# PSUM as one buffer of eight banks, and a new order, in a fused recurrence and feed-forward kernel

## Chip, cores and metric

One NeuronCore of one Trainium2 chip runs the whole kernel. The metric is device time in microseconds. A profiled execution has a span (first to last instruction) and a time of its own, which is a little longer than the span.

## What is computed

Two stages. The first is a recurrence over 768 steps for 4 batches x 8 heads, each with a 40 x 40 state. The second is a feed-forward product on its output, 3072 tokens of 320 features, 2048 wide inside:

```python
for t in range(S):
    y[:, :, t] = einsum('bhd,bhde->bhe', rt, state)
    Sa = einsum('bhde,bhe->bhd', state, at)
    state = state * wt[:, :, None, :] - einsum('bhd,bhe->bhde', Sa, bt)
    state = state + einsum('bhd,bhe->bhde', vt, kt)
...
h = x @ w_in                 # 3072 x 320 by 320 x 2048
g = np.maximum(h, 0.0) ** 2
out = g @ w_out              # 3072 x 2048 by 2048 x 320
```

## The kernel before

The 768 steps are cut into 12 chunks of 64. Within a chunk the recurrence is worked as matrix products; only the state goes from one chunk to the next. For each chunk `c` the kernel plans named steps. The names matter below, since the order is a text of them:

- `prep`: logarithm of the decays (`ln`, `hi`, `lo`), their running sums on PE (`ci`, `cf`) and exponentials of these on ACT (`ei`, `ex`, `ec`, `ef`, `eg`); transposes of the inputs on PE (`TA`, `TR`, `TK`, and `Tk`, `Tb`, `TU` in chunks 0 to 3) with copies or products out of PSUM (`tA`, `tR`, `tK`, ...); the masked score matrix `EN` (PE) and `mEN` (DVE).
- `rec`: `AS`, `EV`, `NU` (PE) with `u0`, `u1` between them solve the chunk; `SC`, `S` and `s` make the new state, `TS` and `tS` turn it.
- `read`: `TV`, `tV`, `CX`, `mCX`, `RS`, `Y`, `y`, `yd`, `XT`, `xt` make the chunk's 256 tokens.
- `ffn`: four quarters `u0` to `u3` of the first product (`F` over 256 of the 320 features, `FL` over the last 64), the Relu `f`, the square `q`, and the second product. For chunks 0 to 10 the second product is four steps `O c u0` to `O c u3`, each of eight matmuls that alternate between the two banks of one buffer, one bank for each half of the tokens; one read `o c` of 640 columns empties both, and `st c` stores. Chunk 11 alone has the halves as steps of their own (`OL 11 u g`, emptied by `oe 11 g`).

PE writes into PSUM, and DVE or ACT must read each result out. PSUM's eight banks are four buffers of two banks each, with tags pb0 to pb3. A PE step that opens a result names its buffer in the order text (`PE3 O 0 u0`; a step that goes on in an open buffer is plain `PE`); everything that reads it goes through `slot` (line 330):

```python
slots[h] = ps.tile([128, 2, 512 if dt == FP32 else 1024], dt, name=f"pb{i}",
                   tag=f"pb{i}", bufs=1)
```

Nothing schedules at run time. `ORDER` (line 82) is one text of some 1050 entries, engine and step, and `Plan.issue` (line 52) emits the instructions in that order; each engine then works through its own in sequence. The framework places the semaphore waits: it compares what the instructions emitted so far read and write in each buffer, and makes a later instruction wait for an earlier one on another engine where the two touch the same part of a buffer and at least one writes, or where both are in PSUM.

The set `WIDE` names transposes and sums done as whole 128 x 128 matmuls; the others are done as pairs of 64-row matmuls that write the two banks of the pair. `flat` (line 499) shows a buffer's two banks as one row for the whole ones, and `sums` (line 505) does so for the exponentials that read `cf`. Entries such as `WD3` are fills: matmuls of constants whose result nobody reads, emitted by `fill` (line 1037).

Of the kernel before, what the change touches and what calls it, by code (L numbers as in the profile page):

```python
# [82 lines left out]
SP ldb 0; PE1 cf 0 h0; ACT castk 0; ACT ln 0 h1; SP lda 0; POOL castb 0; SP ldw 1; SP ldb 1; PE2 Tk
0; DVE hi 0 h1; DVE lo 0 h1; SP ldv 0; PE cf 0 h1; ACT eg 0; POOL castA 0; PE3 WD1; PE3 Tb 0; PE ci
0 h1; DVE tb 0 g0; SP ldk 1; ACT ef 0; ACT ln 1; SP ldr 0; SP lda 1; POOL hi 1; SP ldw 2; DVE tk 0
g0; ACT castb 1; PE1 WD3; PE1 TA 0; POOL lo 1; SP ldk 2; ACT ec 0; DVE tk 0 g1; DVE tb 0 g1; DVE tA
0 g0; DVE tA 0 g1; PE2 WD2; PE3 TU 0; ACT castV 0 g1; PE2 EN 0 g0; DVE mEN 0 g0; PE1 EN 0 g1; PE0
cf 1; POOL castV 0 g0; SP st0 0; POOL castk 1; DVE mEN 0 g1; PE2 ci 1; PE1 EV 0; ACT ec 1; DVE tU
0; PE2 Tb 1; DVE u0 0; PE3 Tk 1; ACT eg 1; PE NU 0; DVE tb 1 g0; POOL castR 0; POOL castA 1; SP ldv
1; ACT ef 1; DVE tb 1 g1; ACT u1 0 g0; SP lda 2; PE0 TR 0; SP ldr 1; ACT u1 0 g1; PE2 TA 1; ACT tR  # L90
0 g0; PE1 S 0 g0; DVE tk 1 g1; DVE tk 1 g0; DVE tA 1 g0; ACT tR 0 g1; PE S 0 g1; ACT ln 2; SP ldw
3; PE3 TV 0; DVE s 0 q1; PE0 EN 1 g0; DVE tA 1 g1; DVE s 0 q0; PE2 TU 1; DVE mEN 1 g0; ACT tV 0; SP
ldb 2; POOL hi 2; PE1 EN 1 g1; POOL lo 2; ACT castk 2; POOL castV 1 g0; DVE tU 1; SP ldv 2; PE3 cf
2; ACT eg 2; ACT ef 2; SP lwi 0 u1; PE0 CX 0 g1; PE2 AS 1; DVE mEN 1 g1; POOL castV 1 g1; PE EV 1;
PE1 CX 0 g0; ACT u0 1; POOL castA 2; PE3 ci 2; DVE mCX 0 g1; PE0 Tk 2; PE NU 1; DVE mCX 0 g0; ACT
ec 2; POOL castR 1; DVE tk 2 g1; DVE tk 2 g0; PE1 TA 2; PE3 TR 1; DVE tA 2 g0; PE0 SC 1; ACT u1 1
g0; POOL castb 2; SP ldk 3; POOL castV 2 g0; SP ldr 2; ACT u1 1 g1; PE2 Y 0; PE S 1 g0; DVE tA 2
g1; ACT ln 3; PE S 1 g1; PE1 TS 0; DVE y 0; DVE yd 0; ACT tR 1 g1; ACT tR 1 g0; DVE s 1 q0; SP ldw
4; SP lwi 0 u0; POOL hi 3; POOL castV 2 g1; DVE s 1 q1; PE2 Tb 2; DVE tb 2 g0; DVE tb 2 g1; PE3 TV
1; PE0 TS 1; PE2 TU 2; ACT tS 0; DVE tS 1; DVE lo 3; SP lwl 0; PE0 EN 2 g0; ACT tV 1; POOL cwi 0  # L100
u1; DVE mEN 2 g0; PE3 EN 2 g1; PE1 cf 3; DVE mEN 2 g1; PE0 CX 1 g1; ACT tU 2; POOL castk 3; PE2 AS
2; POOL castR 2; PE EV 2; PE3 CX 1 g0; ACT eg 3; ACT ef 3; PE1 XT 0; ACT u0 2; DVE mCX 1 g1; PE0 TR
2; PE NU 2; DVE mCX 1 g0; ACT tR 2 g0; PE3 ci 3; POOL cwi 0 u0; DVE xt 0; SP lwi 0 u2; ACT u1 2 g0;
ACT ec 3; PE1 F 0 u1; PE3 RS 1; PE Y 1; SP lwi 0 u3; ACT u1 2 g1; PE2 SC 2; DVE yd 1; PE S 2 g0;
POOL cwl 0; PE S 2 g1; DVE y 1; DVE s 2 q1; ACT tR 2 g1; ACT ln 4; PE3 XT 1; POOL cwi 0 u3; PE FL 0
u1; DVE xt 1; ACT f 0 u1; PE0 TV 2; DVE s 2 q0; ACT tV 2; PE3 Tk 3; PE1 F 1 u0; DVE tk 3 g1; DVE tk
3 g0; SP lda 3; PE2 TS 2; PE FL 1 u0; PE0 CX 2 g0; PE3 FL 0 u2; SP ldb 3; DVE tS 2; SP ldr 3; ACT
cwi 0 u2; DVE mCX 2 g0; PE F 0 u2; POOL hi 4; POOL lo 4; PE2 F 0 u3; SP lwo 0 x0; POOL castb 3; SP
ldv 3; SP lda 4; ACT castA 3; PE0 TA 3; SP lwo 0 x2; PE FL 0 u3; ACT f 1 u0; DVE f 0 u2; ACT f 0
u3; DVE tA 3 g0; POOL castR 3; PE1 FL 1 u2; DVE tA 3 g1; PE3 cf 4; PE F 1 u2; PE0 Tb 3; PE2 FL 1  # L110
u1; SP lwo 0 x1; DVE tb 3 g1; POOL castV 3 g0; ACT ef 4; ACT f 1 u2; POOL cwo 0 x0; POOL castV 3
g1; SP lwo 0 x3; ACT q 0 u2; PE3 CX 2 g1; PE F 1 u1; PE1 F 0 u0; ACT f 1 u1; PE FL 0 u0; DVE tb 3
g0; DVE mCX 2 g1; PE0 FL 1 u3; PE3 EN 3 g0; ACT f 0 u0; ACT q 0 u1; DVE mEN 3 g0; PE2 EN 3 g1; PE F
1 u3; POOL castA 4; SP lwo 0 x6; ACT f 1 u3; SP lwo 0 x5; DVE mEN 3 g1; ACT q 1 u0; PE1 TU 3; PE3
TR 3; PE2 AS 3; PE EV 3; POOL cwo 0 x1; PE0 ci 4 h1; DVE tU 3; DVE q 0 u0; ACT tR 3 g0; PE1 RS 2;
ACT u0 3; PE Y 2; PE NU 3; ACT ei 4 h1; DVE tR 3 g1; DVE y 2; DVE yd 2; ACT u1 3 g0; PE3 O 0 u0; SP
lwo 0 x4; PE1 SC 3; PE S 3 g0; SP lwo 0 x7; POOL q 1 u3; DVE u1 3 g1; PE S 3 g1; ACT ex 4 h1 g0;
DVE s 3 q0; SP ldw 5; PE2 ci 4 h0; DVE s 3 q1; ACT cwo 0 x2; ACT ex 4 h1 g1; POOL cwo 0 x3; SP ldb
4; POOL cwo 0 x6; PE0 XT 2; PE O 0 u1; ACT q 0 u3; SP ldk 4; ACT cwo 0 x4; PE1 TV 3; POOL cwo 0 x7;
ACT cwo 0 x5; ACT ex 4 h0 g1; ACT ei 4 h0; DVE xt 2; PE0 TA 4; PE O 0 u2; ACT ex 4 h0 g0; ACT ln 5;  # L120
PE O 0 u3; DVE tV 3; PE1 CX 3 g0; SP ldv 4; DVE tA 4 g0; DVE tA 4 g1; DVE hi 5; SP lda 5; POOL lo
5; PE0 TS 3; SP ldr 4; POOL mulKB 4 h0; POOL castV 4 g1; POOL castV 4 g0; ACT o 0; DVE mCX 3 g0; SP
lda 6; ACT q 1 u2; PE2 F 2 u0; POOL q 1 u1; PE FL 2 u0; PE1 FL 2 u1; PE F 2 u1; DVE tS 3; POOL
castR 4; ACT f 2 u0; PE0 FL 2 u3; PE2 CX 3 g1; DVE mulKB 4 h1; POOL castA 5; ACT f 2 u1; SP ldb 5;
PE3 ci 5 h1; ACT ei 5 h1; DVE mCX 3 g1; ACT ex 5 h1 g0; ACT ex 5 h1 g1; PE F 2 u3; PE1 TK 4; ACT f
2 u3; PE2 cf 5; ACT ef 5; DVE tK 4; PE3 F 2 u2; PE1 EN 4 g0; PE0 EN 4 g1; DVE mEN 4 g0; POOL q 2
u1; PE FL 2 u2; PE2 O 1 u0; DVE mEN 4 g1; PE1 RS 3; ACT f 2 u2; PE Y 3; PE3 AS 4; SP ldk 5; ACT q 2
u0; PE EV 4; PE O 1 u1; POOL q 2 u3; ACT q 2 u2; DVE yd 3; ACT u0 4; DVE y 3; SP ldw 6; PE1 ci 5
h0; PE0 XT 3; PE NU 4; PE O 1 u2; SP ldk 6; DVE u1 4 g0; PE O 1 u3; ACT ei 5 h0; ACT ex 5 h0 g1;
ACT u1 4 g1; DVE xt 3; PE3 TA 5; PE0 TR 4; ACT ex 5 h0 g0; POOL mulKB 5 h1; ACT o 1; ACT tR 4 g1;  # L130
SP ldr 5; DVE tA 5 g1; PE1 TV 4; PE2 SC 4; POOL mulKB 5 h0; PE S 4 g0; DVE tA 5 g0; PE S 4 g1; ACT
tR 4 g0; ACT ln 6; SP ldv 5; DVE tV 4; PE0 TK 5; DVE s 4 q1; PE3 FL 3 u3; PE F 3 u3; ACT tK 5; PE1
O 2 u0; DVE s 4 q0; ACT hi 6; ACT castR 5; PE0 CX 4 g0; PE2 CX 4 g1; POOL lo 6; SP ldb 6; PE O 2
u1; DVE mCX 4 g0; ACT f 3 u3; PE O 2 u2; ACT castV 5 g0; ACT q 3 u3; DVE mCX 4 g1; PE3 ci 6 h0; SP
st 0; ACT ei 6 h0; PE2 TS 4; PE0 EN 5 g1; ACT ex 6 h0 g0; PE O 2 u3; ACT ex 6 h0 g1; PE3 RS 4; DVE
tS 4; PE Y 4; PE2 EN 5 g0; DVE mEN 5 g1; PE0 cf 6; ACT o 2; PE1 ci 6 h1; DVE y 4; ACT ef 6; POOL
castV 5 g1; ACT ex 6 h1 g0; DVE yd 4; DVE mEN 5 g0; PE3 F 3 u2; PE0 F 3 u1; PE FL 3 u1; ACT ex 6 h1
g1; POOL castA 6; PE FL 3 u2; ACT ei 6 h1; DVE f 3 u1; PE1 XT 4; POOL mulKB 6 h0; PE2 AS 5; ACT f 3
# [942 lines left out]
```

## Time and profile before

| | us |
|---|---|
| three runs | 243.48, 244.87, 242.04 |
| median | 243.48 |
| the profiled execution, its own time | 242.46 |
| its span | 240.6 |
| POOL busy in it | 125.1 |
| squares on POOL (20) | 39.0 |
| squares on ACT (20) | 20.8 |

The page names engines PE (matrix products; PEld is the load of its stationary operand), DVE and ACT (which both read PSUM), POOL (which works in SBUF only) and SP (which issues the loads and stores). In a line of a group, the form is source line, engine, operation, what is written from what, shape, count, then busy time of all of them, the mean duration of one in ns, and the idle time that came just before, with what ended it. Matmuls are pipelined, so their mean duration is longer than their place in a stream, which is busy time by count. In a list of stretches, each row has the busy time of every engine, then the granted PE clock (1.00 is full speed), the share of DMA and its rate.

### The profile page before, as it was taken

How to read it: one execution, taken by the hardware profiler on the slowest of the kernel's cores; microseconds unless marked ns; L12 is line 12 of the kernel's file. 1: busy time of each engine (PE TensorE's matmuls, PEld its weight loads, DVE VectorE, ACT ScalarE, POOL GpSimd, SP SyncE). 2: the span in 40 equal slices, each digit the busy share in tenths (PEclk: the TensorE clock that was granted, in tenths of full speed). 3: DMA queues.
4: the chain of work that ended last, by engine and by line, in shares of the span. 5: the costliest groups of instructions: out<-in, count | busy, mean ns of one | idle time of the engine just before them, and what ended most of it. 6: DMA issues, size and time to landing. Idle time of an engine off the chain costs nothing.

```text
span 240.6 us, 12143 instructions
## 1 busy us (share of the span) xinstructions
PE 223.9 (93%) x5526; PEld 175.8 (73%) x5526; DVE 179.6 (75%) x227; ACT 176.3 (73%) x228; POOL 125.1 (52%) x126
## 2 busy tenths in 40 slices
...
PEclk9999999999999999999999999999999999999998
...
GB/s 99 208 232 180 225 169 207 277 248 177 315 120 174 187 115 172 224 183 158 173 172 151 177 178 178 131 44 126 161 116 6 4 3 23 94 3 3 57 0 108
DMA packets 100873, 33.55 MB, mean 139 GB/s; under 512 B 84950, under 2 KB 100822, under 8 KB 100822
## 3 DMA queue, kind: packets, MB, share of 16 engines
...
q8 instruction: 43, 0.70, 1.2%
...
## 4 chain that ended last, share of the span: by engine, by line
PE 68%; DVE 8%; issue 1%; ACT 1%; DVEq 0%
PE pb L379 36%; PE pb L893 23%; PE pb L383 7%; PE pb L387 2%; DVE STb L796 2%; DVE G L927 1%; DVE AR L679 1%; DVE VUT L360 1%; DVE EN L704 1%; DVE Yb L855 1%; DVE VU L362 1%; DVE CX L704 1%; ACT osb L365 0%; DVE KB L375 0%; ACT lnW L578 0%
## 5 line engine op out<-in xcount | busy, mean ns | idle before, releaser
L379 PE MATMUL pb<-WOUT,G 128*128 128x320 bf16 x384 | 56.8, 300 | 0.0
L929 POOL TENSOR_TENSOR G<-G 128x1024 bf16<-128x1024 bf16 x20 | 39.0, 1958 | 28.3 <-ACT G L921 28.1
L921 ACT ACTIVATE G<-pb 128x1024 bf16<-128x1024 f32 x40 | 40.6, 1022 | 15.4 <-PE pb L893 13.3
L893 PE MATMUL pb<-XT,WIN 128*128 128x256 bf16 x384 | 48.2, 273 | 0.5 <-issue 0.3
L379 PEld LDWEIGHTS <-G 128*128 128x128 bf16 x384 | 35.7, 98 | 14.2 <-issue 0.5
L893 PEld LDWEIGHTS <-WIN 128*128 128x128 bf16 x384 | 35.0, 98 | 8.4 <-issue 2.8
L373 POOL TENSOR_TENSOR KB<-raw_kb,iG 128x640 bf16<-128x640 f32 x14 | 21.7, 1552 | 31.7 <-ACT iG L620 23.7
L704 DVE TENSOR_TENSOR CX<-pb,MSKI 128x1024 bf16<-128x1024 f32 x24 | 28.7, 1218 | 5.8 <-PE pb L379 5.7
L704 DVE TENSOR_TENSOR EN<-pb,MSK 128x1024 bf16<-128x1024 f32 x24 | 28.7, 1217 | 3.8 <-PE pb L379 3.7
L931 ACT ACTIVATE G<-G 128x1024 bf16<-128x1024 bf16 x20 | 20.8, 1051 | 0.1
L796 DVE TENSOR_TENSOR STb<-pb,GT 40x640 bf16<-40x640 f32 x22 | 18.0, 820 | 2.3 <-PE pb L379 2.0
L373 POOL TENSOR_TENSOR lo<-lnW,hi 128x640 bf16<-128x640 f32 x10 | 14.0, 1399 | 9.7 <-ACT hi L365 5.0
L679 DVE TENSOR_TENSOR AR<-pb,GT 128x512 bf16<-128x512 bf16 x24 | 15.6, 684 | 3.2 <-PE pb L383 3.1
L893 PE MATMUL pb<-XT,WLAST 64*128 64x256 bf16 x192 | 17.5, 271 | 0.1
L379 PEld LDWEIGHTS <-EN 64*64 64x64 bf16 x768 | 14.2, 109 | 3.1 <-DVE EN L704 1.3
L923 DVE TENSOR_SCALAR G<-pb 128x1024 bf16<-128x1024 f32 x8 | 9.8, 1220 | 8.7 <-PE pb L893 8.6
L365 ACT ACTIVATE osb<-pb 128x640 f32<-128x640 f32 (+1 forms) x10 | 6.8, 677 | 12.3 <-PE pb L379 10.6
L855 DVE TENSOR_TENSOR Yb<-pb,Gin 128x640 bf16<-128x640 f32 (+1 forms) x24 | 12.4, 553 | 4.3 <-PE pb L379 4.2
L369 POOL CAST VU<-raw_v 64x640 bf16<-64x640 f32 x20 | 14.6, 734 | 1.3 <-DMA raw_v<-in_v_dram 0.7
L626 ACT ACTIVATE Gin<-pb 64x320 f32<-64x320 f32 x32 | 13.7, 428 | 1.5 <-PE pb L379 1.1
L653 ACT ACTIVATE GT<-pb 128x1024 f32<-128x1024 f32 x12 | 12.3, 1022 | 2.4 <-PE pb L379 1.9
L365 ACT ACTIVATE VU<-pb 64x640 bf16<-64x640 f32 x17 | 11.8, 696 | 2.9 <-DVE VU L362 1.6
...
## 6 DMA issues: line engine op xcount, KB each, us to landing
...
```

What stands on the lines that cost most here:

```text
L365: alts.append(("ACT", c_act(n), lambda: nc.scalar.activation(out=o_(), in_=i_(), func=ACTF.Copy, scale=1.0 if scale is None else scale)))
L373: return [("POOL", 40 + 2.35 * n, lambda: nc.gpsimd.tensor_tensor(out=o_(), in0=a_(), in1=b_(), op=op)), ("DVE", c_dve(n), lambda: nc.vect ...
L379: return lambda: nc.tensor.matmul(out=o_(), lhsT=l_(), rhs=r_(), start=start, stop=stop, skip_group_check=True)
L383: return lambda: nc.tensor.transpose(out=o_(), in_=i_(), identity=IDb[64 * g:64 * g + n, 0:n])
L679: ew(f"tA {c} g{g}", [("DVE", c_dve(512), lambda g=g: nc.vector.tensor_tensor(out=steps(AR[q2][:, 0, g]), in0=turned(ha, g), in1=steps(GT[ ...
L704: ew(f"m{nm} {c} g{g}", [("DVE", c_dve(1024), lambda: nc.vector.tensor_tensor(out=dst[q2][:, g].rearrange("p q i t -> p (q i) t"), in0=slo ...
L796: ew(f"s {c} q{q}", [("DVE", c_dve(2 * n), lambda q=q: nc.vector.tensor_tensor(out=STb[q2][live(q), :, q, 0:D], in0=slot(hs, FP32)[live(q) ...
L855: return [("DVE", c_dve(2 * (f1 - f0)), lambda: nc.vector.tensor_tensor(out=Yb[q2][:, :, to:to + f1 - f0], in0=slot(hy, FP32)[:, :, f0:f1] ...
L893: return lambda: nc.tensor.matmul(out=o_(), lhsT=l_(), rhs=r_(), start=begins and opens(hf, x), stop=ends and not opens(hf, x), skip_group ...
L921: ("ACT", c_act(1024), lambda gb=gb, hf=hf: nc.scalar.activation(out=gb, in_=slot(hf, FP32)[:], func=ACTF.Relu)),
L929: ("POOL", 1900, lambda gv=gv: nc.gpsimd.tensor_tensor(out=gv, in0=gv, in1=gv, op=ALU.mult)),
L931: ("ACT", c_act(1024), lambda gv=gv: nc.scalar.activation(out=gv, in_=gv, func=ACTF.Square))],
```

## The change

PSUM becomes one buffer `PB` of eight banks. A step that opens a result names one or two banks by digit: `PE14 CX 3 g1` takes banks 1 and 4, `PE2 OL 1 u0 g1` bank 2 alone. `pick_banks` makes the view, a stride over the bank axis for a pair that lies apart. Chunks 0 to 10 get their second product in halves as chunk 11 had it: `OL c u g`, each half in a bank of its own, and two reads `oe c g` of 320 columns in place of `o c`. Whole transposes of eight blocks fit one bank and take only one. `flat` goes, and views keep the bank as an axis of its own; the exponentials of whole sums (`cf` 0, 2, 3) are read in two halves of 512 columns, by bank. `WIDE` gains TA 3, TA 5, TA 7, TA 8, TR 4 and Tk 2, and loses TA 4, TU 3, TV 3 and cf 1. The order is new throughout, with other engines for some steps (squares: ACT 20 to 14, DVE 8 to 13, POOL 20 to 21; Relu: ACT 40 to 37, DVE 8 to 11; `mulKB` on DVE 2 to 3) and 32 fill matmuls where there were 6. Loads are issued on SP in a new order, and so are the stores.

```diff
-                self.fill(int(where[2:]), name[1], int(name[2:]))
+                self.fill([int(x) for x in where[2:]], name[1], int(name[2:]))
...
-                self.slot_of[h] = int(where[len(eng):])
+                self.slot_of[h] = sorted(int(x) for x in where[len(eng):])
...
+    PB = ps.tile([128, 8, 512], FP32, name="pb", tag="pb", bufs=1)
 
     def slot(h, dt):
 
         if h not in slots:
-            i = plan.slot_of[h]
-            slots[h] = ps.tile([128, 2, 512 if dt == FP32 else 1024], dt, name=f"pb{i}",
-                               tag=f"pb{i}", bufs=1)
-        return slots[h]
+            slots[h] = pick_banks(plan.slot_of[h])
+        return slots[h] if dt == FP32 else slots[h].bitcast(dt)
+
+    def pick_banks(x):
+        return PB[:, x[0]:x[-1] + 1:max(1, x[-1] - x[0]), :]
...
-    def flat(h, dt=BF16):
-        return slot(h, dt)[:].rearrange("p b x -> p (b x)")
+    def block(h, i, dt=BF16):
+        n = 4 if dt == FP32 else 8
+        return slot(h, dt)[:, i // n, 128 * (i % n):128 * (i % n) + 128]
...
+    def exp_sums(c, h, to, scale):
+        def go():
+            if wide_sums(c):
+                for x in range(2):
+                    nc.scalar.activation(
+                        out=to().rearrange("p (g b m) t -> p g b m t", g=2, b=2)[:, :, x],
+                        in_=slot(h, FP32)[:, x].rearrange("p (m g t) -> p g m t", g=2, t=L),
+                        func=ACTF.Exp, scale=scale)
+                return
...
         ho = ("O", c)
-        apart = c == NCH - 1
-
         def bank(g):
-            return slot(ho + (g,), FP32)[:, 0, 0:DM] if apart else slot(ho, FP32)[:, g, 0:DM]
+            return slot(ho + (g,), FP32)[:, 0, 0:DM]
...
-            if apart:
-                for g in range(2):
-                    pe(f"OL {c} u{u} g{g}", "D", DM, ms[g], reads=rd, writes=[ho + (g,)],
-                       alloc=[ho + (g,)] if u == 0 else [])
-            else:
-                pe(f"O {c} u{u}", "D", DM, [m for x in zip(*ms) for m in x], reads=rd,
-                   writes=[ho], alloc=[ho] if u == 0 else [])
+            for g in range(2):
+                pe(f"OL {c} u{u} g{g}", "D", DM, ms[g], reads=rd, writes=[ho + (g,)],
+                   alloc=[ho + (g,)] if u == 0 else [])
...
+        for g in range(2):
+            ew(f"oe {c} g{g}", copy_alts(lambda g=g: osb[q2][:, g, :], lambda g=g: bank(g), DM),
+               reads=[ho + (g,), ("left", c - 2)] + ([("osb", q2)] if c < 2 else []),
+               writes=[("osb", q2, g)], free=[ho + (g,)])
         if c < NCH - 1:
-            ew(f"o {c}", copy_alts(lambda: osb[q2][:], lambda: slot(ho, FP32)[:, :, 0:DM], 2 * DM),
-               reads=[ho], writes=[("osb", q2)], free=[ho])
...
     def fill(i, mode, n):
-        t = ps.tile([128, 2, 512], FP32, name=f"pb{i}", tag=f"pb{i}", bufs=1)
+        t = pick_banks(i)
```

A stretch of the new order, around the second product of chunk 4:

```
PE05 SC 6; PE37 RS 6; PE Y 6; ACT castV 8 g1; PE S 6 g0; PE S 6 g1; PE14 ci 8 h1; PE2 OL 4 u0 g0;
DVE s 6 q1; PE6 OL 4 u0 g1; PE OL 4 u1 g0; DVE y 6; POOL q 4 u2; ACT ex 8 h1 g1; PE OL 4 u1 g1;
ACT ex 8 h1 g0; DVE yd 6; DVE q 5 u3; PE37 cf 8; ACT ei 8 h1; DVE s 6 q0; PE14 ci 8 h0;
DVE mulKB 8 h1; PE05 EN 7 g1; PE OL 4 u2 g1; PE OL 4 u3 g1; ACT ef 8; PE3 TA 8; DVE mEN 7 g1;
ACT ex 8 h0 g0; ACT ex 8 h0 g1; SP ldv 10; SP ldr 9; ACT ei 8 h0; PE OL 4 u2 g0; PE OL 4 u3 g0
```

More of the change, by code (lines that the diff above doesn't have):

```diff
@@ L83 @@
[L83 to L138, printed above, removed]
@@ new lines @@
+WD1; PE ci 0 h1; ACT ln 1; DVE tA 0 g1; DVE tk 0 g0; DVE tk 0 g1; PE7 WD7; PE2 Tb 0; SP ldv 0; DVE
+tb 0 g1; SP lda 1; SP ldb 1; SP ldk 1; DVE tb 0 g0; ACT hi 1; PE7 WD7; PE43 EN 0 g1; POOL lo 1;
+PE27 cf 1; ACT ec 0; DVE tA 0 g0; POOL castA 1; POOL castV 0 g1; PE56 EN 0 g0; ACT castV 0 g0; ACT
+ef 1; PE0 WD1; PE01 TU 0; DVE mEN 0 g1; DVE mEN 0 g0; PE3 TA 1; PE4 WD1; PE56 EV 0; ACT eg 1; SP
+ldr 0; POOL castb 1; ACT u0 0; DVE tA 1 g0; SP ldw 2; SP ldv 1; DVE tU 0; POOL castR 0; PE2 Tb 1;
+DVE tb 1 g1; PE NU 0; DVE tb 1 g0; ACT castk 1; PE0 Tk 1; DVE tA 1 g1; ACT u1 0 g0; ACT u1 0 g1; SP
@@ new lines @@
+ldb 2; PE17 ci 1; PE4 WD2; PE56 S 0 g0; ACT ec 1; PE S 0 g1; ACT ln 2; ACT hi 2; DVE tk 1 g0; DVE
+tk 1 g1; DVE s 0 q0; PE32 EN 1 g0; POOL lo 2; SP ldr 1; POOL castb 2; POOL castV 1 g1; PE1 TR 0; SP
+ldk 2; DVE s 0 q1; ACT tR 0 g1; PE07 TV 0; PE45 EN 1 g1; SP ldw 3; ACT tR 0 g0; PE61 TU 1; SP lda
+2; DVE mEN 1 g0; POOL castR 1; PE23 cf 2; ACT tV 0; POOL castk 2; DVE mEN 1 g1; DVE tU 1; PE07 CX 0
+g1; PE45 CX 0 g0; PE16 AS 1; ACT castV 1 g0; PE EV 1; ACT eg 2; DVE mCX 0 g1; PE0 Tb 2; POOL castA
@@ new lines @@
+u1; PE F 0 u1; ACT f 0 u2; DVE tA 3 g1; DVE tk 3 g1; PE01 TS 2; POOL castb 3; DVE xt 1; PE23 F 1
+u0; ACT f 0 u1; PE45 CX 2 g0; ACT cwi 0 u3; PE FL 1 u0; SP lwo 0 x2; SP lwo 0 x0; DVE tk 3 g0; DVE
+tA 3 g0; PE76 CX 2 g1; DVE tS 2; ACT ln 4; PE01 FL 0 u3; DVE mCX 2 g0; DVE mCX 2 g1; PE F 0 u3;
+PE45 F 1 u2; ACT hi 4; ACT f 0 u3; POOL lo 4; PE FL 1 u2; DVE f 1 u0; POOL castV 3 g0; ACT q 0 u1;
+PE67 Tb 3; DVE tb 3 g1; SP ldr 3; PE01 cf 4; POOL cwo 0 x3; ACT ef 4; PE23 F 0 u0; PE FL 0 u0; DVE
+tb 3 g0; ACT f 1 u2; SP lwo 0 x5; PE01 EN 3 g0; SP lwo 0 x4; DVE mEN 3 g0; PE67 F 1 u1; PE45 EN 3
@@ new lines @@
+u1; PE14 TK 4; DVE tS 3; DVE tK 4; ACT f 2 u1; PE Y 3; SP lda 5; POOL q 1 u0; PE03 F 2 u2; DVE y 3;
+PE14 EN 4 g0; PE67 EN 4 g1; POOL hi 5; PE FL 2 u2; DVE yd 3; POOL lo 5; PE2 OL 1 u0 g1; SP ldk 5;
+DVE mEN 4 g0; PE5 OL 1 u0 g0; POOL castV 4 g1; PE OL 1 u1 g0; ACT f 2 u2; POOL castV 4 g0; PE03 ci
+5 h1; POOL castA 5; SP ldb 5; PE14 XT 3; ACT q 2 u0; PE OL 1 u2 g0; SP ldw 6; DVE mEN 4 g1; ACT ex
+5 h1 g0; DVE xt 3; ACT ex 5 h1 g1; ACT ei 5 h1; PE67 AS 4; PE EV 4; ACT u0 4; ACT castR 4; PE03 ci
@@ new lines @@
+g1; PE OL 2 u2 g1; PE37 F 3 u3; DVE mCX 4 g1; PE25 CX 4 g0; ACT tS 4; SP lda 6; PE FL 3 u3; POOL lo
+6; PE14 ci 6 h0; PE OL 2 u2 g0; SP ldb 6; PE OL 2 u3 g1; ACT f 3 u3; ACT ei 6 h0; DVE mCX 4 g0; PE
+OL 2 u3 g0; PE37 EN 5 g1; PE25 cf 6; DVE oe 2 g1; DVE oe 2 g0; ACT ex 6 h0 g0; ACT ex 6 h0 g1; ACT
+ef 6; PE61 RS 4; DVE mEN 5 g1; SP ldw 7; PE Y 4; PE40 ci 6 h1; SP ldv 6; ACT ex 6 h1 g0; PE25 F 3
+u2; POOL castA 6; DVE y 4; DVE yd 4; POOL castR 5; PE FL 3 u2; ACT ex 6 h1 g1; ACT ei 6 h1; PE16 FL
@@ new lines @@
+POOL hi 7; POOL lo 7; DVE tV 5; PE OL 3 u2 g0; PE1 OL 3 u0 g1; SP ldk 7; PE62 ci 7 h0; DVE s 5 q0;
+DVE s 5 q1; PE37 EN 6 g1; PE54 CX 5 g0; DVE q 3 u3; DVE mEN 6 g1; PE OL 3 u1 g1; PE OL 3 u3 g0;
+POOL castV 6 g1; ACT ei 7 h0; PE37 cf 7; ACT ex 7 h0 g1; ACT ex 7 h0 g0; ACT oe 3 g0; DVE mCX 5 g0;
+PE26 EN 6 g0; ACT castV 7 g0; POOL castA 7; PE OL 3 u2 g1; PE4 TA 7; PE50 FL 4 u3; SP lda 8; POOL q
+4 u0; SP ldv 8; ACT ef 7; DVE mEN 6 g0; PE37 ci 7 h1; ACT ln 8; DVE tA 7 g0; ACT ei 7 h1; PE26 CX 5
@@ new lines @@
+h1; PE05 EN 7 g1; PE OL 4 u2 g1; PE OL 4 u3 g1; ACT ef 8; PE3 TA 8; DVE mEN 7 g1; ACT ex 8 h0 g0;
+ACT ex 8 h0 g1; SP ldv 10; SP ldr 9; ACT ei 8 h0; PE OL 4 u2 g0; PE OL 4 u3 g0; SP lda 10; POOL
+mulKB 8 h0; DVE tA 8 g0; ACT ln 9; DVE tA 8 g1; PE14 AS 7; PE EV 7; SP ldb 9; ACT oe 4 g1; PE36 XT
+6; PE05 TK 8; ACT oe 4 g0; ACT hi 9; ACT xt 6; DVE u0 7; DVE tK 8; PE27 TR 7; ACT tR 7 g1; PE NU 7;
+POOL castA 9; PE36 F 6 u1; ACT u1 7 g0; ACT u1 7 g1; DVE tR 7 g0; PE05 EN 8 g1; PE27 FL 6 u0; DVE q
+5 u0; ACT castR 8; PE FL 6 u1; DVE mEN 8 g1; PE14 TV 7; PE F 6 u0; PE05 SC 7; ACT f 6 u1; ACT f 6
@@ new lines @@
+u0; PE S 7 g0; PE S 7 g1; SP ldk 9; SP ldw 10; POOL castV 9 g1; DVE tV 7; PE36 FL 6 u2; PE14 FL 6
+u3; PE27 EN 8 g0; PE F 6 u2; DVE s 7 q0; PE F 6 u3; DVE s 7 q1; DVE mEN 8 g0; PE05 TS 7; DVE tS 7;
+POOL lo 9; POOL castA 10; ACT f 6 u2; ACT f 6 u3; PE36 TS 6; PE27 AS 8; PE EV 8; PE05 ci 9 h1; ACT
+tS 6; PE14 TR 8; POOL castV 10 g1; DVE u0 8; ACT ex 9 h1 g1; PE3 OL 5 u0 g0; ACT ln 10; SP st 4;
+POOL q 5 u2; DVE tR 8 g1; PE6 OL 5 u0 g1; ACT ei 9 h1; POOL q 6 u2; PE NU 8; DVE tR 8 g0; PE OL 5
+u1 g0; PE OL 5 u2 g0; POOL castR 9; PE OL 5 u1 g1; DVE u1 8 g0; PE OL 5 u2 g1; ACT u1 8 g1; PE27 CX
@@ new lines @@
+PE OL 6 u2 g1; POOL mulKB 9 h1; DVE tA 9 g1; SP ldv 11; POOL lo 10; DVE s 8 q0; PE14 CX 8 g1; PE23
+TK 9; PE67 XT 7; PE OL 6 u3 g1; ACT tK 9; DVE xt 7; PE OL 6 u3 g0; DVE mCX 8 g1; PE67 F 7 u2; PE14
+EN 9 g0; PE FL 7 u2; PE23 ci 10 h1; DVE oe 6 g1; ACT oe 6 g0; PE05 RS 8; SP ldr 11; SP ldk 11; ACT
+ln 11; ACT f 7 u2; ACT ex 10 h1 g1; PE Y 8; PE67 F 7 u0; DVE mEN 9 g0; DVE y 8; DVE yd 8; ACT ei 10
+h1; PE FL 7 u0; ACT ex 10 h1 g0; PE05 ci 10 h0; PE23 EN 9 g1; ACT ex 10 h0 g0; DVE f 7 u0; PE14 F 7
```

213 lines of the change are left out of this document (114 added, 99 removed).

## The prediction

> **What bounds the kernel now.** I read the page's busy shares first, then the chain that ended last, then the busy time by stretch.
>
> ```profile
> span 240.6 us, 12143 instructions
> ...
> PE 223.9 (93%) x5526; PEld 175.8 (73%) x5526; DVE 179.6 (75%) x227; ACT 176.3 (73%) x228; POOL 125.1 (52%) x126
> ...
> PEclk9999999999999999999999999999999999999998
> ...
> PE 68%; DVE 8%; issue 1%; ACT 1%; DVEq 0%
> ```
>
> ```profile
> 0.00:5.00 5.00, 0.00 (x0) 0.00 (x0) 3.80 (x16) 1.70 (x2) 4.28 (x17) 1.00 0.41 90
> 140.00:160.00 20.00, 19.17 (x590) 15.50 (x590) 17.32 (x19) 15.00 (x21) 12.11 (x10) 1.00 0.64 133
> 180.00:200.00 20.00, 19.89 (x556) 14.91 (x554) 15.66 (x19) 13.93 (x19) 12.39 (x11) 1.00 0.02 5
> 235.00:240.60 5.60, 1.07 (x8) 0.54 (x6) 0.49 (x1) 0.44 (x1) 0.00 (x0) 0.87 0.43 116
> ```
>
> The first numbers after each stretch are its length, then PE, PEld, DVE, ACT and POOL busy. PE carries the end: it is busy 19 to 20 of every 20 us between start and tail, and it stays so because DVE and ACT empty PSUM (16 and 14 of 20 us) *at the same time as each other and as PE*. PE's idle time is 240.6 - 223.9 = 16.7 us, of which 5 lie before the first load and 4.5 behind 235; no DMA stands in the chain. So this kernel has about 7 us to win and lives from three engines overlapping. The question for any change is whether they still may.
>
> **What the change does to the waits.** Before, PSUM is four buffers of two banks, and a wait can only join steps that use the same buffer. After, it is one buffer, and a pair may be two banks that lie apart: the order text gives 137 steps a pair apart (41 of them banks 1 and 4, 19 banks 0 and 5), 87 a pair side by side and 42 one bank. A matmul writes one bank, but the instruction that empties a pair apart is a strided view from the first bank to the last. I went through the waits of both built programs. In the changed one, 160 waits between PE and an emptying engine, and 110 between ACT and DVE, join two instructions that share no bank and no other data; in all 270 the spans from first to last bank overlap, and no wait joins steps whose spans are disjoint. In the program before I find nothing of the kind. So the built order treats banks 1 and 4 as 1 to 4. Four neighbours from chunk 3, banks in brackets:
>
> ```
> PE  OL 0 u0 g0 -> [4]      waits for   DVE s 3 (first)  <- [2,5]
> DVE s 3 (second) <- [2,5]  waits for   PE  OL 0 u0 g0 -> [4]
> ACT oe 0 g0 <- [4]         waits for   DVE s 3 (second) <- [2,5]
> DVE xt 2 <- [2,5]          waits for   ACT oe 0 g0 <- [4]
> ```
>
> Not one of the four has a bank in common. What is queued behind each waiting instruction on its engine waits as well, since the queues keep the order of the text.
>
> On this the Trainium skill ("PSUM — Partial Sum Buffer", section "PSUM bank collisions raise a hardware error") speaks for the idea of the change: it asks that engines be kept apart by bank and quadrant, so disjoint banks need no order. The chip would allow the overlap; the built program forbids it, and no run here shows the chip's side.
>
> **The price, on one stretch.** Rows for the durations:
>
> ```profile
> L379 PE MATMUL pb<-WOUT,G 128*128 128x320 bf16 x384 | 56.8, 300 | 0.0
> L893 PE MATMUL pb<-XT,WIN 128*128 128x256 bf16 x384 | 48.2, 273 | 0.5 <-issue 0.3 <-DVE AR L679 0.2
> L379 PE MATMUL pb<-AR,VUT 64*128 64x64 bf16 x384 | 8.8, 190 | 1.0 <-DVE VU L362 0.7
> L387 PE MATMUL pb<-IDQ,VU 128*128 128x128 bf16 x64 | 4.2, 219 | 0.0
> L1044 PE MATMUL pb<-UTI 128*128 128x512 bf16 x6 | 2.7, 541 | 0.0
> L921 ACT ACTIVATE G<-pb 128x1024 bf16<-128x1024 f32 x40 | 40.6, 1022 | 15.4 <-PE pb L893 13.3 <-issue 2.0
> L620 ACT ACTIVATE iG<-pb 128x640 f32<-128x640 f32 x16 | 11.2, 701 | 2.9 <-PE pb L379 2.7
> L626 ACT ACTIVATE Gin<-pb 64x320 f32<-64x320 f32 x32 | 13.7, 428 | 1.5 <-PE pb L379 1.1
> L365 ACT ACTIVATE VUT<-pb 128x2048 bf16<-128x2048 bf16 x5 | 9.4, 1875 | 0.1
> L365 ACT ACTIVATE AR<-pb 128x512 bf16<-128x512 bf16 x16 | 9.0, 596 | 2.4 <-PE pb L383 1.6 <-PE pb L387 0.3 <-DVE AR L360 0.3
> L365 ACT ACTIVATE osb<-pb 128x640 f32<-128x640 f32 x9 | 6.3, 704 | 6.3 <-PE pb L379 4.5 <-issue 1.1 <-DMA out_dram<-osb 0.7
> L365 ACT ACTIVATE osb<-pb 128x320 f32<-128x320 f32 x1 | 0.4, 437 | 6.0 <-PE pb L379 6.0
> L704 DVE TENSOR_TENSOR CX<-pb,MSKI 128x1024 bf16<-128x1024 f32 x24 | 28.7, 1218 | 5.8 <-PE pb L379 5.7
> L796 DVE TENSOR_TENSOR STb<-pb,GT 40x640 bf16<-40x640 f32 x22 | 18.0, 820 | 2.3 <-PE pb L379 2.0
> L679 DVE TENSOR_TENSOR AR<-pb,GT 128x512 bf16<-128x512 bf16 x24 | 15.6, 684 | 3.2 <-PE pb L383 3.1
> L360 DVE COPY VUT<-pb 128x2048 bf16<-128x2048 bf16 x7 | 8.5, 1219 | 1.9 <-PE pb L383 1.3 <-PE pb L387 0.7
> ```
>
> Busy time by count gives a matmul's place in a stream (56.8 / 384 = 0.148 us for the second product, 0.1255 for the first); the mean is how long the last one takes to land. For the small ones the stream rate is read from a single step, and the hand-overs from pieces of the chain:
>
> ```profile
> 128.24 0.39 PE L893 MATMUL pb<-XT,WLAST 64*128 64x256 bf16 x4
> 128.47 0.63 PE L379 MATMUL pb<-AR,VUT 64*128 64x64 bf16 x32
> ```
>
> ```profile
> 7.57 0.47 ACT L578 ACTIVATE lnW<-raw_w 128x320 f32<-128x320 f32 x1 [0.92 <-DMA raw_w<-in_w_dram]
> ```
>
> ```profile
> 131.75 0.02 issue
> 131.77 1.23 DVE EN L704
> ...
> 135.66 1.14 DVE EN L704
> 136.80 0.04 issue
> 136.84 0.41 PE pb L383 x16
> ...
> 236.11 0.44 ACT osb L365
> ```
>
> 32 matmuls in 0.63 us, less 0.19 for the last to land, is 0.0145 each; four of WLAST to the next step's start is 0.23, 0.0575 each; a hand-over is 0.02 to 0.04, I take 0.03. The third load lands at 7.6.
>
> Now walk the changed order from y 6 (DVE, banks 3 and 7) to the third quarter of OL 4. Each line waits for the one above it: y 6 0.82; OL 4 u1 g1 in bank 6, 4 matmuls, 3 x 0.148 + 0.30 = 0.74; yd 6 [3,7] 0.29; cf 8 [3,7] 31 x 0.0145 + 0.19 = 0.64; ei 8 h1 (ACT, [1,4]) 0.70; s 6 (DVE, [0,5]) 0.82; ci 8 h0, EN 7 g1, 8 matmuls of OL 4, together 0.27 + 0.23 + 7 x 0.148 + 0.30 = 1.84; ef 8 (ACT, [3,7]) 1.02; TA 8 in bank 3, 7 x 0.058 + 0.22 = 0.63; mEN 7 g1 (DVE, [0,5]) 1.22; ex, ex and ei 8 h0 (ACT, [1,4]) 0.43 + 0.43 + 0.70; then PE may go on. That is 10.3 us, with 10 hand-overs 10.6, of which PE issues or lands 3.9. Before, 10 us hold 9.6 to 10 us of PE (the stretches above).
>
> **The whole sum.** The same addition from the first instruction to the last store, every instruction starting when the one ahead on its engine and all that the built program makes it wait for are done, gives one heaviest chain:
> - 8.2 to the first read: it waits for raw_a, now the fourth load.
> - DVE 120.5: CX and EN 36 x 1.218 = 43.8; STb and Yb 22 x 0.82 = 18.0; KBT and AR 22 x 0.684 = 15.0; VUT and KBT copies 11 x 1.22 = 13.4; the rest 30.3.
> - ACT 94.4: Relu 25 x 1.022 = 25.6; iG 13 x 0.70 = 9.1; VU and NZ, 640 columns too, 16 x 0.70 = 11.2; VUT and KBT 6 x 1.875 = 11.3; Gin 17 x 0.43 = 7.3; the rest 29.9.
> - PE 119.6 while it issues: OL 238 x 0.148 = 35.2; F 234 x 0.1255 = 29.4; 2406 small ones x 0.0148 = 35.7; FL 113 x 0.0575 = 6.5; the rest 12.8; and 89 times the last matmul's landing, 0.24 on the mean, 21.3.
> - 231 hand-overs x 0.03 = 6.9; from the end of the last read of PSUM to the span's end 240.6 - 236.55 = 4.0.
>
> Sum 374.9. The same addition over the order before gives 243.0 against 240.6 measured, so I take off 2.4: span 372.5. The profiled run was 242.46, 1.9 over its span, and lies 1.0 under the median of the three runs; I forecast **374 us**. 168 of the 231 hand-overs on that chain are waits without a bank in common, or reads that only share one. With all such waits left out the addition gives 246.8.
>
> **The other edits** are inside that sum or small. 26 more fill matmuls, at 0.126 to 0.45 each (the rows of 256 columns and of the six fills; I take 0.21) are 5.5 us of PE, 11 of them ahead of the first real matmul, one on the chain. The split of O into OL moves no matmul: 320 columns and 0.148 stay; 11 reads of 640 columns become 22 of 320, 11 x (2 x 0.437 - 0.704) = +1.9 over DVE and ACT. Six exponentials cut in halves: 6 x (2 x 0.596 - 1.022) = +1.0 on ACT. Six transposes become whole ones, at 8 x 0.066 against 16 x 0.023, +0.2 each, and three other steps go back: under 1 us either way. ACT gives six squares away, DVE takes five. Loads are issued in a new order on SP; no DMA stood in the chain, and a longer span gives them more room.
>
> **Rivals.**
> 1. *The waits cost nothing* (not slower): what is waited for is long done whenever it is asked. Then 246.8 - 2.4 + 1.9 = 246, or down to 241 if the order fills some of the 7 us of PE's idle time. Against it: the 168 hand-overs carry 374.9 - 246.8 = 128.1 us, 0.76 each, and it decides only if that falls under 15 ns each (2.4 us, 1% of 243, about what can be told from no change here). Chance 0.05.
> 2. *Only ACT and DVE run in line*, PE works under them. The chain through their instructions alone, with overlapping spans in order, is 333 instructions and 270.2 us; with 5 us before the first, 89 changes of engine x 0.03 and the tail of 4.1 that is 282, and 284 as a run. Reached only if PE's waits on spans never come last; up to 345. Chance 0.10.
> 3. *PE's clock falls.* PE would issue for 216 of 374 us, 58%, in bursts, the longest pause of the addition 3.2 us. The first quoted stretch shows 1.00 over 5 us without a matmul, the last one 0.87 with PE busy 1.07 of 5.60. If the granted clock went to half throughout, PE's issue on the chain could double: 374 + 120 = 494; a part of it 400 to 490. Chance 0.12. The Trainium skill ("TensorE: Matmul & The Clock Gate", section "A second HAM failure mode: psum-queue depth-cycling") tells of a kernel in which short idles between matmul groups made the clock go to half and back; the first row above is not like it, the last might be.
> 4. *The changed program doesn't order by span on the chip.* The waits stand in the program that is built, so this is inside rival 1.
>
> **How the numbers follow.** The forecast takes 0.73. Its own range: hand-overs at 0.02 or 0.05 move it by -2 to +5; instructions that follow on the same engine start about 0.08 early (1.14 against 1.23 above), some 107 on the chain, -9; DMA landings and code that I can't see, +20. So 355 to 395. To hold 8 in 10 the range goes down into rival 2 and up into rival 3: 345 to 425. Faster by over 1% 0.02, within 1% 0.03, slower 0.95.
>
> **What would show it.** PE busy near 60%; idle time of ACT ended by DVE and of DVE by ACT, tens of us each where the page before has hardly any; the chain's shares near DVE 33%, ACT 25%, PE 38%; PE's waits on ACT and DVE at steps whose banks differ; the granted clock still 1.00. PE busy above 85% would refute the sum, a clock of 0.8 or less speak for rival 3, and a chain with little PE for rival 2.

## The result, and the profile after

The changed kernel takes 418.44 us (median of 4 runs, 416.91 to 422.68) where the kernel before takes 244.18 (4 runs, 242.04 to 245.71): a ratio of 1.72, 95% interval 1.70 to 1.74. The forecast was 374 with a range from 345 to 425, so the direction and the range held, and the number itself lay 44 us low. The narrower range that the prediction gives for its own sum, 355 to 395, did not hold: the measured time lies in the part of the range that had been added for rival 3.

The page of the changed kernel, the parts that answer to those quoted of the kernel before:

```profile
span 416.7 us, 12259 instructions
...
PE 290.0 (70%) x5560; PEld 209.6 (50%) x5560; DVE 192.7 (46%) x245; ACT 174.0 (42%) x234; POOL 119.5 (29%) x119
...
PEclk9988689999599755899656855659597789888999
...
PE 50%; DVE 22%; ACT 17%; issue 5%; SPq 2%; DMA 1%; POOL 1%; DVEq 0%; ACTq 0%; POOLq 0%
...
L394 PE MATMUL pb<-WOUT,G 128*128 128x320 bf16 x384 | 70.2, 340 | 10.7 <-ACT iG L644 3.3
L943 ACT ACTIVATE G<-pb 128x1024 bf16<-128x1024 f32 x37 | 37.4, 1023 | 85.2 <-PE pb L915 24.7
L915 PE MATMUL pb<-XT,WIN 128*128 128x256 bf16 x384 | 64.6, 324 | 8.3 <-DVE EN L726 1.5
...
L726 DVE TENSOR_TENSOR CX<-pb,MSKI 128x1024 bf16<-128x1024 f32 x24 | 29.2, 1223 | 32.8 <-PE pb L915 8.9
```

Read it from the right end of each group. What one instruction of DVE or ACT takes has not moved: 1023 ns for the Relu and 1223 for the masked triangle, against 1022 and 1218 before. What stands in front of them has: ACT idles 85.2 us ahead of its Relus (15.4 before), DVE 32.8 ahead of the CX triangles (5.8 before). The chain, which was PE for 68%, now passes through PE, DVE and ACT in turn. And one thing is there that the sum did not hold: the second-product matmul grew from 56.8 to 70.2 us for the same 384, the first from 48.2 to 64.6, and the row PEclk, nines before but for its last digit, has fives and sixes. The mean granted clock is 0.811.

The view of the waits of the changed kernel, each row with the waiting engine and line, the one waited for, the total in us, how often, and the longest:

```profile
ACT G L943 <- DVE EN L726: 14.3, 3, 9.6
...
PE pb L394 <- ACT G L943: 10.6, 10, 2.1
...
PE pb L394 <- DVE CX L726: 10.1, 9, 1.5
ACT G L943 <- DVE Sb L375: 9.9, 1, 9.9
DVE VUT L375 <- ACT G L943: 9.2, 2, 5.6
```

The largest row between ACT and DVE in the same view of the kernel before:

```profile
DVE VU L362 <- ACT iG L620: 2.3, 1, 2.3
```

Between ACT and DVE no data pass in the rows of the changed kernel: ACT's Relu of the FFN has no use for DVE's masked EN or its state copy Sb, nor DVE's copy to VUT for the Relu. (L394 on PE is the line of many steps; its rows hold waits for data too.) Added up over the 197 rows that the view gives of the changed kernel (the smallest 0.3 us) and the 103 of the kernel before, ACT and DVE wait for each other 175.4 us (8.4 in the kernel before) and PE waits for the two 115.6 us (10.6 before).

The stretch that the prediction walked, from y 6 to the point where PE may go on, is in the chain of the changed kernel (start, us, what):

```profile
225.52 0.84 DVE Yb L877
...
226.40 0.72 PE pb L394 x4
...
227.21 0.30 DVE Yb L877
...
227.55 0.64 PE pb L394 x31
...
228.26 0.71 ACT iG L644
...
229.00 0.83 DVE STb L818
...
229.87 1.89 PE pb L394 x28
...
231.78 1.03 ACT GT L531
...
232.85 0.62 PE pb L402 x8
...
233.57 1.24 DVE EN L726
...
235.72 0.71 ACT iG L644
...
236.48 3.93 PE pb L394 x32
```

The pieces come in the order of the walk, one engine at a time, 236.48 - 225.52 = 10.96 us against 10.6. Here the matmul pieces still have their full-clock length (0.72, 0.64, 1.89 against 0.74, 0.64, 1.84). Elsewhere many have not, as the two products above show; what that adds is worked out below.

### The profile page after: what moved, and what is told of

It is laid out like the page before. It is cut to its first block, busy times and chain, and to the rows that moved or that the text cites. A ratio compares the mean times of both kernels' runs of the same rounds, so it can differ in the third digit from the quotient of the medians.

```text
span 416.7 us, 12259 instructions
## 1 busy us (share of the span) xinstructions
PE 290.0 (70%) x5560; PEld 209.6 (50%) x5560; DVE 192.7 (46%) x245; ACT 174.0 (42%) x234; POOL 119.5 (29%) x119
## 4 chain that ended last, share of the span: by engine, by line
PE 50%; DVE 22%; ACT 17%; issue 5%; SPq 2%; DMA 1%; POOL 1%; DVEq 0%; ACTq 0%; POOLq 0%
PE pb L394 26%; PE pb L915 14%; PE pb L398 6%; ACT G L943 5%; DVE CX L726 4%; DVE EN L726 4%; PE pb L1059 2%; DVE Yb L877 2%; DVE STb L818 2%; DVE G L945 2%; ACT iG L644 2%; PE pb L402 2%; DVE VUT L375 1%; ACT VU L380 1%; ACT VUT L380 1%
## 5 line engine op out<-in xcount | busy, mean ns | idle before, releaser
L394 PE MATMUL pb<-WOUT,G 128*128 128x320 bf16 x384 | 70.2, 340 | 10.7 <-ACT iG L644 3.3
L943 ACT ACTIVATE G<-pb 128x1024 bf16<-128x1024 f32 x37 | 37.4, 1023 | 85.2 <-PE pb L915 24.7
L915 PE MATMUL pb<-XT,WIN 128*128 128x256 bf16 x384 | 64.6, 324 | 8.3 <-DVE EN L726 1.5
L394 PEld LDWEIGHTS <-G 128*128 128x128 bf16 x384 | 40.3, 109 | 32.9 <-issue 11.6
L915 PEld LDWEIGHTS <-WIN 128*128 128x128 bf16 x384 | 41.0, 113 | 24.3 <-issue 13.5
L726 DVE TENSOR_TENSOR CX<-pb,MSKI 128x1024 bf16<-128x1024 f32 x24 | 29.2, 1223 | 32.8 <-PE pb L915 8.9
L726 DVE TENSOR_TENSOR EN<-pb,MSK 128x1024 bf16<-128x1024 f32 x24 | 29.1, 1223 | 24.3 <-PE pb L394 6.7
L915 PE MATMUL pb<-XT,WLAST 64*128 64x256 bf16 x192 | 21.4, 314 | 13.3 <-DVE G L945 2.1
L877 DVE TENSOR_TENSOR Yb<-pb,Gin 128x128 bf16<-128x128 f32 (+1 forms) x24 | 13.0, 556 | 25.6 <-PE pb L394 11.8
L388 POOL TENSOR_TENSOR lo<-lnW,hi 128x640 bf16<-128x640 f32 x11 | 15.4, 1397 | 31.9 <-ACT hi L380 31.0
L394 PEld LDWEIGHTS <-EN 64*64 64x64 bf16 x768 | 17.2, 124 | 5.3 <-issue 2.4
L375 DVE COPY VUT<-pb 128x2048 bf16<-128x2048 bf16 x8 | 9.8, 1221 | 19.2 <-ACT G L943 9.2
L915 PEld LDWEIGHTS <-WLAST 64*128 64x128 bf16 x192 | 8.9, 104 | 18.3 <-issue 16.4
L394 PE MATMUL pb<-AR,VUT 64*128 64x64 bf16 x384 | 10.4, 198 | 10.1 <-DVE Sb L375 2.1
L380 ACT ACTIVATE osb<-pb 128x320 f32<-128x320 f32 x14 | 6.1, 434 | 25.4 <-PE pb L394 19.1
```

Source lines behind the costliest of these rows:

```text
L380: alts.append(("ACT", c_act(n), lambda: nc.scalar.activation(out=o_(), in_=i_(), func=ACTF.Copy, scale=1.0 if scale is None else scale)))
L388: return [("POOL", 40 + 2.35 * n, lambda: nc.gpsimd.tensor_tensor(out=o_(), in0=a_(), in1=b_(), op=op)), ("DVE", c_dve(n), lambda: nc.vect ...
L394: return lambda: nc.tensor.matmul(out=o_(), lhsT=l_(), rhs=r_(), start=start, stop=stop, skip_group_check=True)
L726: ew(f"m{nm} {c} g{g}", [("DVE", c_dve(1024), lambda: nc.vector.tensor_tensor(out=dst[q2][:, g], in0=slot(hb, FP32)[:].rearrange("p q (i t ...
L877: return [("DVE", c_dve(2 * (f1 - f0)), lambda: nc.vector.tensor_tensor(out=Yb[q2][:, :, to:to + f1 - f0], in0=slot(hy, FP32)[:, :, f0:f1] ...
L915: return lambda: nc.tensor.matmul(out=o_(), lhsT=l_(), rhs=r_(), start=begins and opens(hf, x), stop=ends and not opens(hf, x), skip_group ...
```

## The experiments

Five readings were set against each other. **S**: the waits by the span of two banks apart make the loss. **B**: the one buffer, its views and the exponentials in halves cost by themselves. **O**: the new order is poor. **C**: PE's work in the new order lowers the clock by itself. **W**, later: what the filler matmuls do. "The addition" is that of the prediction, over the program of each kernel.

**1. One buffer, pairs side by side.** The order text, the wide set and the FFN of the kernel before, put into the changed kernel's buffer. The line that matters, against the changed kernel:

```diff
-    def pick_banks(x):
-        return PB[:, x[0]:x[-1] + 1:max(1, x[-1] - x[0]), :]
+    def pick_banks(i):
+        return PB[:, 2 * i:2 * i + 2, :]
```

> The order, the wide set and the whole (not halved) second FFN product of the kernel before, in the one buffer of eight banks, each old buffer as two banks side by side (0 and 1, 2 and 3, ...). Theory S (the waits by the span of two banks apart make the loss): no pair is apart, the addition of the prediction over this program gives 242.2 against 243.0 for the kernel before, so 241 to 246 us, clock 1.00, PE busy about 93%. Theory B (one buffer with views of it, and the exponentials in two halves, cost by themselves): 260 or more. Theories O (the new order) and C (the clock falls by the new order's PE work) also say 241 to 246.

Measured: 244.12 us (10 runs), ratio to the kernel before 1.0016 (0.9961 to 1.007), span 242.8, clock 0.993:

```profile
PE 224.9 (93%) x5526; PEld 177.3 (73%) x5526; DVE 180.9 (75%) x227; ACT 177.1 (73%) x236; POOL 125.5 (52%) x126
```

One buffer costs nothing that can be told from no change. B falls.

**2. The same with pairs four apart.** One more line:

```diff
-        return PB[:, 2 * i:2 * i + 2, :]
+        return PB[:, i:i + 5:4, :]
```

> As the side-by-side kernel, with one line changed: old buffer i is now banks i and i+4, so that the span of every pair covers a bank of every other pair, while no step shares a bank that it did not share before. Theory S: the addition gives 502.5, so 500 us at full clock; with a clock that falls as in the changed kernel (its 416.7 against 372.5) up to 570; PE busy below 60%. Theory O: 244, since the order is the old one. Theory C: 244 with clock 1.00. Theory B: the same as the side-by-side kernel.

Measured: 616.67 us (one run), clock 0.636. The page:

```profile
span 615.0 us, 12214 instructions
...
PE 366.4 (60%) x5526; PEld 255.8 (42%) x5526; DVE 185.7 (30%) x227; ACT 180.7 (29%) x236; POOL 124.2 (20%) x126
...
PEclk9555656766665656665557585665766566666689
```

The instructions, their order and which steps share a bank are those of experiment 1; the bank numbers alone are spread. That costs 372 us, in one run, where four runs of the changed kernel lie within 6 us of each other: the old order, fast with pairs side by side, is 2.5 times as long with pairs apart. O and B would have it at 244. It also is 47 us over S's upper end, 570: what a lower clock adds had been taken too small there as well.

**3. The changed kernel, reading by bank.** Where a pair lies apart, one instruction becomes two of one bank each, on DVE and ACT. `by_bank` does this, and `apart` tells where. The rest of the edit, left out here, holds `apart`, calls `act`, `copy`, `vts` and `vtt` in place of the engines' own calls and gives the operands of `s` the bank as an axis:

```diff
...
+    def by_bank(op):
+        def go(out, **kw):
+            x = kw["in_"] if "in_" in kw else kw["in0"]
+            for b in (slice(0, 1), slice(1, 2)) if apart(x) else (slice(0, 2),):
+                op(out=out[:, b] if apart(x) else out,
+                   **{k: v[:, b] if apart(x) and k in ("in_", "in0", "in1") else v
+                      for k, v in kw.items()})
+        return go
+    act, copy = by_bank(nc.scalar.activation), by_bank(nc.vector.tensor_copy)
+    vts, vtt = by_bank(nc.vector.tensor_scalar), by_bank(nc.vector.tensor_tensor)
...
```

> The changed kernel, order, banks and all, with each read of a pair apart issued as two instructions of one bank each (137 steps have such a pair); the built program then has no wait left between instructions that share neither bank nor data. Theory S: the addition gives 254.2 (246.8 without those waits, and some 7 for the additional instructions), so 248 to 265 us, granted clock back to 0.98 or more. Theory O: 380 to 430, since the order is the new one. Theory C: the clock stays near 0.81 and the time lies over 280, since PE's work and its order are those of the changed kernel.

Measured: 244.55 us (10 runs), ratio to the kernel before 1.0031 (0.9983 to 1.0079), clock 1.000. The page:

```profile
span 242.3 us, 12500 instructions
...
PE 227.1 (94%) x5560; PEld 176.6 (73%) x5560; DVE 197.1 (81%) x334; ACT 176.4 (73%) x302; POOL 120.1 (50%) x119
...
PEclk9999999999999999999999999999999999999999
```

This kernel does *more* than the changed one, 157 instructions on DVE and ACT (334 + 302 against 245 + 234), with the same order, banks, fillers and halved second product, and is 174 us shorter. The waits of ACT and DVE for each other are back at 9.2 us and those of PE for both at 3.6; the largest row between ACT and DVE is now:

```profile
ACT AR L360 <- DVE AR L360: 2.2, 2, 2.0
```

The clock is full with the same fillers as in the changed kernel. O and C fall. The addition's 254 was too high by 9.5 us in the span. It held 7.4 for the second reads (254.2 - 246.8), which DVE and ACT may well do beside PE; the rest is not explained, and neither part was tried alone.

**4. The banks renamed, common pairs as neighbours.**

```diff
-                self.fill([int(x) for x in where[2:]], name[1], int(name[2:]))
+                self.fill([BANK[int(x)] for x in where[2:]], name[1], int(name[2:]))
...
-                self.slot_of[h] = sorted(int(x) for x in where[len(eng):])
+                self.slot_of[h] = sorted(BANK[int(x)] for x in where[len(eng):])
...
+BANK = (3, 0, 7, 6, 1, 2, 4, 5)
```

> The changed kernel with the eight banks given other numbers throughout (0 to 7 become 3, 0, 7, 6, 1, 2, 4, 5), which makes the commonest pairs neighbours: which steps share a bank is unchanged, but instructions that read a pair apart fall from 137 to about 80 steps. Theory S: the addition gives 305.3 against 374.9, so 303 us at full clock and up to 340 with a clock that falls by part. Theory O and theory C: 418 as the changed kernel, since nothing that they speak of is different. Theory B: 418.

Measured: 317.17 us (one run), clock 0.945:

```profile
span 315.5 us, 12272 instructions
...
PE 246.2 (78%) x5560; PEld 187.7 (59%) x5560; DVE 190.5 (60%) x245; ACT 173.8 (55%) x234; POOL 120.0 (38%) x119
...
PEclk9987889999999999997776999998899999999999
```

101 us go with a change of names. Waits of ACT and DVE for each other are 91.4 us, about half.

**5. The banks renamed, common pairs far apart.** The same edit with BANK = (3, 7, 2, 6, 1, 5, 4, 0). By then three spans had shown what the clock adds to the addition, so that it could be forecast here.

> The converse of the renamed kernel: the changed kernel with its banks 0 to 7 called 3, 7, 2, 6, 1, 5, 4, 0, which puts the commonest pairs far apart; which steps share a bank is unchanged again. Theory S: the addition gives 458.3 (374.9 as changed, 305.3 with the commonest pairs as neighbours), and on top the stretch of PE's work by a lower clock, which was 12.6 us at 0.945, 44 at 0.811 and 115 at 0.636: at about 0.70 some 85 us, so 500 to 560 us with 540 the likeliest. Theory O (the order): 418.

Measured: 542.9 us (one run), clock 0.704:

```profile
span 541.2 us, 12274 instructions
...
PE 344.6 (64%) x5560; PEld 239.6 (44%) x5560; DVE 193.0 (36%) x245; ACT 175.6 (32%) x234; POOL 118.6 (22%) x119
```

The addition and the stretch by the clock, one on top of the other, gave 540. The clock that this used, about 0.70, was itself put between the 0.811 and 0.636 of two runs.

**6. Reading by bank with the banks renamed.** Experiment 3 with BANK = (2, 1, 4, 5, 0, 3, 7, 6), so that fewer pairs lie apart.

> The kernel that reads pairs apart by bank, with banks 0 to 7 called 2, 1, 4, 5, 0, 3, 7, 6, so that only 69 steps instead of 137 need the second read. Theory S1 (with exact waits PE alone sets the time, as its 94% busy says): the same as the kernel with 137 second reads, 242 to 246 us. Theory S2 (the second reads on DVE and ACT, 15 us of busy time in all, still cost on the chain): 3 to 6 us less, 238 to 241, by the addition 248.3 against 254.2.

Measured: 243.37 us (12 runs), ratio to the kernel before 0.9981 (0.994 to 1.0021), span 242.4, PE busy 228.0. DVE and ACT give up 5.1 us of work (193.7 + 174.7 against 197.1 + 176.4) and the span stays: S1. The expectation's "15 us" for the second reads was too much; experiment 3 shows 6.8 more than the changed kernel (4.4 on DVE, 2.4 on ACT), to about 1 us: DVE does the same work in experiment 7 in 198.1.

**7. Reading by bank without the fillers.**

```diff
             if name[0] == "W":
-                self.fill([int(x) for x in where[2:]], name[1], int(name[2:]))
                 continue
```

> The kernel that reads pairs apart by bank, without the filler matmuls (32 of 128x512 in 8 places, all in the first 55 us but one; they compute nothing that is used). Theory S1 with fillers that PE pays for: PE busy falls by about 7 us (32 x 0.2135) from 227 and the time by 3 to 6, to 239 to 242. Theory W (the eleven fillers ahead of the first product warm the clock, and the others lie in waits for loads): PE's first products run at half clock as in the kernel before, and the time stays or rises by 1 to 3 us, 244 to 248.

Measured: 245.8 us (12 runs), ratio to the kernel before 1.0061 (1.0026 to 1.0096), PE busy 224.3. PE gives up 2.8 us of work, not 7, and the time does not fall: W. A part of the reason is to be seen in PE's first rows. First without, then with the eleven fillers (start, us, instructions):

```profile
5.69 0.42 PE L407 MATMUL pb<-hi,UTB 128*128 128x320 bf16 x1 [5.69 <-DVE hi L359]
...
6.43 0.31 PE L407 MATMUL pb<-UTB,hi 128*128 128x128 bf16 x1
6.54 0.31 PE L407 MATMUL pb<-UTB,lo 128*128 128x128 bf16 x1
```

```profile
4.67 3.85 PE L1074 MATMUL pb<-UTI 128*128 128x512 bf16 x11 [4.67 <-POOL UTI L272]
8.35 0.30 PE L408 MATMUL pb<-hi,UTB 128*128 128x320 bf16 x1
...
8.84 0.22 PE L408 MATMUL pb<-UTB,hi 128*128 128x128 bf16 x1
8.89 0.22 PE L408 MATMUL pb<-UTB,lo 128*128 128x128 bf16 x1
```

Without fillers the first products start 2.7 us earlier and follow each other at 0.11 us; with them at 0.05 to 0.06. What PE pays for the fillers it gets back, at least in part, on what follows. The kernel before, with no fillers ahead of its first products, starts slowly too: eight matmuls of 128 columns take 1.06 us at 7.21 and 0.61 at 21.26, and the clock column of the stretch that holds the first reads 1.00:

```profile
7.21 1.06 PE L387 MATMUL pb<-IDQ,KB 128*128 128x128 bf16 x8
...
21.26 0.61 PE L387 MATMUL pb<-IDQ,tA 128*128 128x128 bf16 x8
```

```profile
5.00:10.00 5.00, 3.74 (x27) 2.94 (x28) 1.43 (x3) 1.73 (x4) 3.83 (x7) 1.00 0.87 203
```

So a 1.00 in that column early in a profile does not show that PE runs at full speed.

**8. Experiment 6 with the first eleven fillers alone.**

> The renamed kernel that reads by bank, with the first eleven fillers kept and the other 21 left out. Theory W: as the kernel with all of them within 1%, 242 to 246. Theory S1 with fillers that PE pays for: 2 to 4 us less, 239 to 242, which would be below both kernels.

Measured: 244.85 us (12 runs), ratio to the kernel before 1.0028 (0.9992 to 1.0063). W again. No version beat the kernel before by more than can be told: the five that are free of the waits by span lie at 0.998 to 1.006 of it, with PE busy 92 to 94%.

## Why the prediction was right, and where it was short

**What bounds the kernel, and what the change does to it: right.** Experiment 3 takes the waits by span away, at the price of second reads, and the loss is gone to within 0.8%. Experiments 2, 4 and 5 put them in, halve them and add to them by bank numbers alone, and the time follows each time. The Trainium skill ("PSUM — Partial Sum Buffer", section "PSUM bank collisions raise a hardware error") was cited for disjoint banks needing no order; experiment 3, which orders by single bank, has PE busy 94%, DVE 81% and ACT 73% of 242.3 us, so the trace agrees. It is the order in the built program that forbade the overlap.

**The sum: the waits were priced well, the clock was not in it.** The addition less 2.4, as the prediction takes it, against the spans. The last column is PE's busy time at full clock (227.1 in experiment 3, 224.9 in experiment 1) times (1/clock - 1), the stretch of PE's work if all of it ran at the mean clock:

| kernel | addition - 2.4 | span | difference | clock | PE's stretch |
|---|---|---|---|---|---|
| 1, side by side | 239.8 | 242.8 | 3.0 | 0.993 | 1.6 |
| 3, read by bank | 251.8 | 242.3 | -9.5 | 1.000 | 0 |
| 4, renamed, near | 302.9 | 315.5 | 12.6 | 0.945 | 13.2 |
| the changed kernel | 372.5 | 416.7 | 44.2 | 0.811 | 52.9 |
| 5, renamed, far | 455.9 | 541.2 | 85.3 | 0.704 | 95.5 |
| 2, four apart | 500.1 | 615.0 | 114.9 | 0.636 | 128.7 |

In the four kernels with waits by span the difference is 0.84 to 0.95 of the stretch. The step that was short is "PE 119.6 while it issues", with its 21.3 for landings: these are full-clock durations, and "the granted clock still 1.00" was expected. The chain has PE at 50% of 416.7, 208 us, where the sum had 119.6 + 21.3 = 141. So the forecast's mechanism came together with a part of rival 3, which had been given 400 to 490 and a chance of 0.12 as something apart. It isn't apart: the waits that put PE in line also cut its work into bursts, and in these runs the clock goes down with them. Experiments 1 and 2 show that the clock follows the waits (0.993 and 0.636 with the same matmuls in the same order). That it *costs* the 44 us rests first on a fit through four kernels and one forecast made with it (540 for 542.9). The trace gives an estimate without the fit: take the PE pieces of the chain and multiply each by (1 - the granted clock at its time). In the changed kernel this makes 50 of 211 us, in experiment 4 12.5 of 170, against differences of 44.2 and 12.6. It counts as if every part of a piece stretched with the clock, so it may be somewhat high. No run held the clock up with the waits in place.

Two smaller things in the prediction do not stand. The terms given for the sum's own range (-2 to +5, -9, +20) make 363 to 399 around 374, not 355 to 395; neither holds 418, so it was the allowance for rival 3 that kept the measured time inside the range. And rival 3 weighs a granted clock of 1.00 over the first 5 us, without a matmul; since that column reads 1.00 early on while PE runs slowly (experiment 7), the row decides nothing.

**The signs it named.** PE busy "near 60%" is 70%: 227 us of full-clock work would be 54%, the clock stretched it to 290. ACT's idle time ended by DVE and DVE's by ACT, "tens of us each": 89.5 and 85.9 over the view of the waits, where it has 2.9 and 5.5 for the kernel before. The chain's shares near 33, 25 and 38% for DVE, ACT and PE came out as 22, 17 and 50: where PE is stretched, the chain may go through it more often; this was not tried.

**Rival 1** asked for waits that cost under 15 ns each; taking them away was worth 174 us. **Rival 2**, DVE and ACT in line with PE below them, did not come: PE waits 115.6 us for the two. The addition over the changed program gives 306.8 with the waits between ACT and DVE alone and 332.2 with PE's alone, so both kinds count in the calculation; they were not tried singly on the chip.

**The other edits: right.** Halved second product, 26 more fillers, six more exponentials, new wide set and new order of loads are all in experiment 3, together at 1.0031 (0.9983 to 1.0079). The order without the waits by span had been put at 246; it runs 244.55. The 5.5 us of fillers were 2.8 in PE's busy time for all of them, and free in the end.
